# Attention by a forward and a backward running product in place of one and its inverse, in a fused attention and two-layer kernel with a planned order

## The chip, the cores and the metric

One core of one Trainium2 chip runs the whole program. The metric is device time in microseconds, the median of the runs shown; the profile is one execution more. TensorE is called PE here, VectorE DVE, ScalarE ACT, GpSimd POOL, and SP is the queue that issues the transfers.

## The reference

Attention with a decaying state (4 batches, 8 heads, 768 steps, head width 48), then two feed-forward layers over 3072 tokens of width 384, with 1536 and 2048 hidden columns:

```python
for t in range(S):
    cur = np.einsum('bhd,bhe->bhde', u[None] * kt, vt)
    y[:, :, t] = np.einsum('bhd,bhde->bhe', rt, state + cur)
    state = wt[:, :, :, None] * state + np.einsum('bhd,bhe->bhde', kt, vt)
...
a = x @ w_a
b = x @ w_b
x = (a * b) @ w_out
h = np.maximum(x @ w_in, 0.0)
return h * h @ w_out2
```

## The kernel before

**Attention.** 64 steps are a chunk, two chunks of one batch are a pair: 24 pairs, `p0` to `p23`. Transposed r, k and w of a pair lie on 48 + 48 of 112 partitions, one row for each channel and, along the row, 8 heads of 64 steps. `at_scan` (L248) makes the running product of w along each chunk, in `ef`; `at_recip` (L253, four instructions) its inverse, in the second part of `ef`. `at_kr` (L257) multiplies k by the inverse, `at_rr` (L261, one instruction for each chunk) r by the product. From these PE makes the scores `sc` (`at_A`, L288) and the transposed keys `kt` (`at_B`, L299), ACT copies them to `kn`, and PE makes the state update `ds` (`at_C`, L311). `at_C2` (L320 to L324, four steps on DVE) adds the old state and multiplies by the product over the whole chunk, once for each chunk. The bonus term u goes on the diagonal: two multiplications of `nat` (L270), a sum (`at_u2`, L274) and `at_diag` (L278, two). `at_A2` (L294) copies the scores under a mask over it. `at_D` (L332) is the output product `yp`; ACT copies it to `ys`, and it is stored to DRAM as `xd`.

**Feed-forward.** Every product is three float32r products of high and low parts. Layer 1 has 12 weight units, called u0 to u11 here, each 1152 columns for the parts a, b and out of one step f; layer 2 has 11. A unit comes as 64-bit words and is decoded in place: ACT two passes (`dec_z`, `dec_round`), DVE `dec_sign` (L191), `dec_shift` (L195), `dec_add` (L200), ACT `dec_hi`, then `dec_lo` (L209), after which PE may use it. The buffers `z` between these are two. A block of tokens (layer 1: 384, 256, 384, then 512) is loaded as x and split in two (`xl`, L551). Then, for each f: PE makes a and b (`pa`, L358 to L360), ACT copies a, DVE multiplies (L369), ACT takes the high part `gh`, POOL the low part `gl` (L379), and PE adds the step's part into three accumulators `acc` (L385 to L387).

**What sets the order.** `Plan.run` places every step by its due time (`prio`), its costs (`t_dve`, `t_pool`, ...), its needs and the free buffers, and the steps are then issued in this order; each engine and the SP queue works through its own list in order, and semaphores hold what isn't ready. The numbers in `KNOB` set the due times and `ENG` the engines a step may take: `kr`, `gl`, `dg` and `u1` are POOL's, `rr`, `da` (`dec_add`) and `dl` (`dec_lo`) DVE's or POOL's. In the plan POOL's steps and the DVE steps marked `port` exclude each other. Pairs p0 to p2 are block 0 of layer 1, p3 and p4 block 1.

Of the kernel before, what the change touches and what calls it, by code (L numbers as in the profile page):

```python
# [31 lines left out]
T0 = 4
TR, TK, TN = T0, T0 + HC, T0 + 2 * HC
EN = HE + HC
WS = 256.0

KNOB = dict(START=13.52, FIRST=7.12, LEAD=18.8, DEC=4.0, DO=13.32, XO=5.1, X2=-14.73, D2=33.64, LW=15.56, LT=19.97,
            LV=-2.26, LV2=-0.35, LN=7.51, scan=2.25, rec=6.21, kr=-1.09, rr=5.02, u1=-0.24, u2=2.9, dg=-11.72,
            gd=-27.44, A=-3.1, B=4.87, C=-16.56, D=10.05, T2=4.14, EARLY=2.77, WAIT=0)
# [84 lines left out]
def fused_kernel(ctx, tc, tpk, natpk, vpk, v2pk, upk, cst, w1pk, w2pk, out):  # L124
# [319 lines left out]
    def plan_pair(p):  # L444
# [16 lines left out]
        add("scan", {"DVE": 1.27}, K["scan"], lambda e: at_scan(p), [("LT", p)], port=True)
        for k in range(4):
            add(("rec", k), {"DVE": 0.87}, K["rec"] - k, lambda e, k=k: at_recip(p, k), [("scan", p)])
        add("kr", both(0, HC, *ENG["kr"]), K["kr"], lambda e: at_kr(p, e), [("LRK", p), *((("rec", k), p) for k in range(4))],
            port=True)
# [390 lines left out]
```

## Time and profile before

| | |
|---|---|
| median of 3 runs | 999.94 us (999.16 to 1000.58) |
| profiled execution | 998.08 us, span 996.2 us |
| mean granted clock of TensorE | 0.976 |
| PE, DVE, ACT, POOL busy | 940.4 (94%), 479.3 (48%), 384.1 (39%), 441.6 (44%) us |
| chain that ended last, by engine | PE 88%, DVE 5%, DMA 3% |

Busy time is what an engine spent in instructions, matmuls with a modelled end. Stretches with different limits lie under these shares, so the rows further down go by stretch: start-up and first pairs, block 0, and the rest. A row's start less the start before it is the pace of an engine; its own duration is some 0.08 us longer, since instructions overlap at their ends. An entry in brackets is the idle time before an instruction and what ended it.

### The profile page before, as it was taken

The numbers are of one execution on the slowest core, as the hardware profiler recorded it, in microseconds if no ns is written. First come the engines' busy times: TensorE is split into PE (matmuls) and PEld (weight loads), VectorE is DVE, ScalarE is ACT, GpSimd is POOL, SyncE is SP. The second block draws the span as 40 slices with busy tenths as digits, with TensorE's granted clock in tenths as the row PEclk, the third lists the DMA queues.
The fourth block names the chain that finished last, engine by engine and source line by source line (L and its number), as shares of the span: only waits on it lengthen the run. The fifth ranks groups of instructions, "written<-read, shape, count | busy, mean of one in ns | idle before, by whom it ended". The sixth has DMA issues, their size and how long they took to land.

```text
span 996.2 us, 14962 instructions
## 1 busy us (share of the span) xinstructions
PE 940.4 (94%) x5982; PEld 802.0 (81%) x5982; DVE 479.3 (48%) x585; ACT 384.1 (39%) x591; POOL 441.6 (44%) x359
## 2 busy tenths in 40 slices
PE   2668799999999999999999999999999999999997
PEld 2567699999988888888888888888888888888885
DVE  6889988875764444573212688721121211211111
ACT  1677443433422333332332677442233332323322
POOL 6733478886674545544122344333333333333332
PEclk9579899999999999999999999999999999999999
DMA  9995134652632332341111554010010000100001
GB/s 267 335 332 135 59 99 128 178 148 77 166 117 76 108 107 77 94 135 38 40 42 64 191 205 143 1 64 1 6 59 0 33 32 1 64 1 1 32 0 37
DMA packets 57791, 91.89 MB, mean 92 GB/s; under 512 B 23664, under 2 KB 31600, under 8 KB 57712
## 3 DMA queue, kind: packets, MB, share of 16 engines
q1 hardware_dynamic: 57712, 90.84, 29.6%
q8 instruction: 49, 0.80, 0.3%
q14 instruction: 30, 0.25, 0.1%
HBM read 76.66 MB, written 14.16 MB: 91 GB/s over the span
## 4 chain that ended last, share of the span: by engine, by line
PE 88%; DVE 5%; DMA 3%; ACT 1%; issue 1%; SPq 0%; POOL 0%; DVEq 0%; ACTq 0%
PE pa L358 16%; PE pa L360 16%; PE pa L359 16%; PE acc L385 11%; PE acc L387 11%; PE acc L386 11%; PE sc L288 2%; PE yp L332 2%; DVE w L209 1%; DVE z L200 1%; PE kt L299 1%; DMA ef<-in_tpk_dram 1%; PE ds L313 1%; DVE z L195 1%; DMA vs<-in_vpk_dram 1%
## 5 line engine op out<-in xcount | busy, mean ns | idle before, releaser
L379 POOL TENSOR_TENSOR gl<-a,gh 128x512 fp32r<-128x512 f32 (+2 forms) x180 | 235.2, 1308 | 474.4 <-ACT gh L176 469.9
L358 PE MATMUL pa<-xh,w 128*128 128x512 f32 (+2 forms) x792 | 296.3, 374 | 7.7 <-ACT w L176 3.3
L360 PE MATMUL pa<-xh,w 128*128 128x512 f32 (+2 forms) x792 | 295.1, 373 | 7.6 <-DVE w L209 7.6
L359 PE MATMUL pa<-xl,w 128*128 128x512 f32 (+2 forms) x792 | 294.4, 372 | 0.0
L365 ACT ACTIVATE a<-pa 128x512 f32<-128x512 f32 (+2 forms) x180 | 102.3, 569 | 277.8 <-PE pa L360 219.1
L385 PE MATMUL acc<-gh,w 128*128 128x512 f32 (+2 forms) x540 | 205.6, 381 | 0.0
L387 PE MATMUL acc<-gl,w 128*128 128x512 f32 (+2 forms) x540 | 202.7, 375 | 0.0
L386 PE MATMUL acc<-gh,w 128*128 128x512 f32 (+2 forms) x540 | 202.4, 375 | 0.0
L369 DVE TENSOR_TENSOR a<-a 128x512 f32<-128x512 f32 x96 | 67.9, 707 | 253.4 <-ACT a L365 253.4
L176 ACT ACTIVATE gh<-a 128x512 fp32r<-128x512 f32 (+2 forms) x180 | 108.3, 602 | 207.7 <-DVE a L369 161.9
L358 PEld LDWEIGHTS pa<-xh,w 128*128 128x128 f32 x792 | 150.1, 190 | 32.8 <-ACT w L176 4.3
L360 PEld LDWEIGHTS pa<-xh,w 128*128 128x128 f32 x792 | 150.2, 190 | 32.0 <-DVE w L209 9.2
L359 PEld LDWEIGHTS pa<-xl,w 128*128 128x128 f32 x792 | 150.1, 189 | 22.7 <-DVE xl L551 0.3
L369 DVE TENSOR_TENSOR a<-a,pa 128x512 f32<-128x512 f32 (+2 forms) x84 | 51.0, 607 | 140.8 <-PE pa L360 140.4
L385 PEld LDWEIGHTS acc<-gh,w 128*128 128x128 f32 x540 | 101.4, 188 | 17.9
L387 PEld LDWEIGHTS acc<-gl,w 128*128 128x128 f32 x540 | 101.5, 188 | 17.3 <-POOL gl L379 0.4
L386 PEld LDWEIGHTS acc<-gh,w 128*128 128x128 f32 x540 | 101.5, 188 | 16.2
L253 DVE RECIPROCAL ef<-ef 112x128 f32<-112x128 f32 x96 | 82.7, 913 | 0.5
L261 POOL TENSOR_TENSOR ar<-rk,ef 48x512 f32<-48x512 f32 (+1 forms) x48 | 59.0, 1230 | 27.8 <-DVE ef L248 10.0
L294 DVE COPY_PREDICATED ar<-mask,sc 64x512 f32<-64x512 int32 x48 | 35.2, 734 | 39.7 <-PE sc L289 37.7
L278 POOL TENSOR_TENSOR ar<-ident,dg 64x512 f32<-64x512 f32 x48 | 51.5, 1073 | 1.8
L209 DVE TENSOR_TENSOR w<-z,w 128x1152 fp32r<-128x1152 f32 (+1 forms) x22 | 37.2, 1691 | 6.0 <-ACT w L176 6.0
(54 smaller groups left out, 834.3 us busy)
## 6 DMA issues: line engine op xcount, KB each, us to landing
raw<-in_w1pk_dram SPq DMA_DIRECT2D x36, 384.0 KB, 6.8
raw<-in_w2pk_dram SPq DMA_DIRECT2D x32, 384.0 KB, 3.8
rk<-in_tpk_dram SPq DMA_DIRECT2D x24, 448.0 KB, 4.9
nat<-in_natpk_dram SPq DMA_DIRECT2D x24, 384.0 KB, 3.7
v<-in_v2pk_dram SPq DMA_DIRECT2D x24, 384.0 KB, 4.3
ef<-in_tpk_dram SPq DMA_DIRECT2D x24, 227.5 KB, 3.7
vs<-in_vpk_dram SPq DMA_DIRECT2D x48, 96.0 KB, 2.8
xd<-ys SPq DMA_DIRECT2D x48, 96.0 KB, 3.2
```

Of the source, the lines that this page charges most:

```text
L176: nc.scalar.activation(out=out, in_=in_, func=ACTF.Copy, **({} if scale is None else {"scale": scale}))
L253: nc.vector.reciprocal(out=hv(inv(p), C)[:, h0:h0 + 2], in_=hv(ext(p), C + 1)[:, h0:h0 + 2, 1:])
L261: eng(e).tensor_tensor(out=hv(AR[p % 2][rows, c, :], C), in0=hv(RK[p][rows, TR:TK], C), in1=hv(ext(p), C + 1)[rows, :, 0:C], op=ALU.mult)
L358: nc.tensor.matmul(out=out, lhsT=blk(wh, k), rhs=h, start=(k == 0), stop=False)
L359: nc.tensor.matmul(out=out, lhsT=blk(wh, k), rhs=l, start=False, stop=False)
L360: nc.tensor.matmul(out=out, lhsT=blk(wl, k), rhs=h, start=False, stop=(k == KD - 1))
L365: nc.scalar.activation(out=a[:, 0:n], in_=P[:, 0:n], func=func, scale=scale)
L369: eng(e).tensor_tensor(out=a[:, 0:n], in0=a[:, 0:n], in1=b[:, 0:n], op=ALU.mult)
L379: eng(e).tensor_tensor(out=gl[:, 0:n], in0=g[:, 0:n], in1=gh[:, 0:n], op=ALU.subtract)
L385: nc.tensor.matmul(out=o, lhsT=blk(wh, d), rhs=gh[:, 0:n], start=first, stop=False)
L386: nc.tensor.matmul(out=o, lhsT=blk(wl, d), rhs=gh[:, 0:n], start=False, stop=False)
L387: nc.tensor.matmul(out=o, lhsT=blk(wh, d), rhs=gl[:, 0:n], start=False, stop=last)
```

## The change

- The inverse goes. The host sends w a second time, reversed in each chunk, and k, v and the rows of the scores are reversed too. `at_scan` makes two running products, `bwd` and `fwd`, with one small reciprocal between them (of the product over a whole chunk, 8 columns), which starts the forward one. `at_kr` multiplies k by `bwd`. The load of `ef` is 112x1040 in place of 112x520.
- `at_C2` has three steps in place of four; the multiplication of the incoming state is a step of its own, `at_Z`, in place.
- In pairs p0 to p5 (`ENG0`) `kr`, `rr`, `dg` and `u1` are DVE's; the additions `da` of layer 1 are DVE's too. Later pairs keep them on POOL.
- Due times are new, with one for each of p0 to p7, and some steps wait for the same step of the pair before. Block 0 could be computed in two parts, which is off (`APART=0`).

```diff
-EN = HE + HC
+EN = 2 * HE
...
 ENG = dict(kr=("POOL",), da=("DVE", "POOL"), dl=("DVE", "POOL"), rr=("POOL", "DVE"), u2=("DVE",), xs=("DVE",), d2=("ACT",),
-           b2=("ACT",), gl=("POOL",), gh=("ACT",))
+           b2=("ACT",), gl=("POOL",), gh=("ACT",), dg=("POOL",), u1=("POOL",), ds=("DVE",))
+ENG0 = dict(ENG, kr=("DVE",), da=("DVE",), rr=("DVE",), dg=("DVE",), u1=("DVE",))
+NP0 = 6
...
     def at_load(p):
         EF[p] = ap.tile([112, EN], F32, tag="ef", name="ef", bufs=3)
-        nc.sync.dma_start(out=ext(p), in_=tpk[p, :, 2 * HC:])
+        nc.sync.dma_start(out=EF[p], in_=tpk[p, :, 2 * HC:])
...
     def at_scan(p):
-        nc.vector.tensor_tensor_scan(out=ext(p), data0=ext(p), data1=floor[0:112], initial=0.0,
+        first = hv(floor, C + 1)[:, :, 0:1]
+        nc.vector.memset(first[0:112], 1.0)
+        nc.vector.tensor_tensor_scan(out=bwd(p), data0=bwd(p), data1=floor[0:112], initial=0.0,
                                      op0=ALU.mult, op1=ALU.max)
-
-    def at_recip(p, q):
-        h0 = q * 2
-        nc.vector.reciprocal(out=hv(inv(p), C)[:, h0:h0 + 2], in_=hv(ext(p), C + 1)[:, h0:h0 + 2, 1:])
+        nc.vector.reciprocal(out=first[0:112], in_=whole(p))
+        nc.vector.tensor_tensor_scan(out=fwd(p), data0=fwd(p), data1=floor[0:112], initial=0.0,
+                                     op0=ALU.mult, op1=ALU.max)
...
+    def at_Z(p):
+
+        v = VS[p % 2][EV, 0, :]
+        if p % PPB == 0:
+            nc.vector.memset(v, 0.0)
+        else:
+            nc.vector.tensor_tensor(out=hv(v, D), in0=hv(v, D), in1=whole(p)[EV].to_broadcast([D, H, D]), op=ALU.mult)
+
     def at_C2(p):
...
-        nc.vector.tensor_tensor(out=P[EV], in0=P[EV], in1=vs[EV, 0, :], op=ALU.add)
-        nc.vector.tensor_tensor(out=hv(vs[OD, 1, :], D), in0=hv(P[EV], D), in1=fe[EV], op=ALU.mult)
+        z = vs[OD, 1, :]
+        nc.vector.tensor_tensor(out=z, in0=P[EV], in1=vs[EV, 0, :], op=ALU.add)
+        nc.vector.tensor_tensor(out=hv(z, D), in0=hv(z, D), in1=whole(p)[OD].to_broadcast([D, H, D]), op=ALU.mult)
         if p % PPB != PPB - 1:
-            nc.vector.tensor_tensor(out=P[OD], in0=P[OD], in1=vs[OD, 1, :], op=ALU.add)
-            nc.vector.tensor_tensor(out=hv(nx[EV, 0, :], D), in0=hv(P[OD], D), in1=fe[OD], op=ALU.mult)
+            nc.vector.tensor_tensor(out=nx[EV, 0, :], in0=P[OD], in1=z, op=ALU.add)
...
-        if j == 0:
-            q = K["FIRST"] * (i - m)
-        else:
-            q = tau[j - 1] + (tau[j] - tau[j - 1]) * i / m - K["LEAD"]
+        E0 = ENG0 if p < NP0 else ENG
+        q = K.get(f"P{p}", tau[j - 1] + (tau[j] - tau[j - 1]) * i / m - K["LEAD"] if j else 0.0)
...
-        add(("da", u, s), {"DVE": t_dve(n) + 0.08, "POOL": t_pool(n)}, prio, lambda e: dec_add(u, n, e), [("dt", u, s)],
+        add(("da", u, s), both(0, n, *(ENG0 if s == 1 else ENG)["da"]), prio, lambda e: dec_add(u, n, e), [("dt", u, s)],
```

What this does to the order is shown at three places. The first is pair p0, from the first scan on. Before, on DVE (`ef` is the pair's products, `dg` the diagonal, `vs_91` state and v):

```order
L248 SCALAR_TENSOR_TENSOR ef<-ef,floor 112x520 x2
L253 RECIPROCAL ef<-ef 112x128 x4
L274 TENSOR_REDUCE dg<-nat 128x8
L253 RECIPROCAL ef<-ef 112x128 x4
L319 MEMSET vs_91 48x384
```

and, beside it, on POOL (`rk` is r and k of a pair, `ar_89` and `ar_90` the score rows of two pairs):

```order
L270 TENSOR_TENSOR nat<-nat 128x384
L270 TENSOR_TENSOR nat<-nat,u_sb 128x384
L261 TENSOR_TENSOR ar_89<-rk,ef 48x512
L261 TENSOR_TENSOR ar_89<-rk,ef 64x512
L257 TENSOR_TENSOR rk<-rk,ef 112x512
```

Now all of it stands in DVE's list, one after the other:

```order
L263 MEMSET floor 112x8
L264 SCALAR_TENSOR_TENSOR ef<-ef,floor 112x520
L266 RECIPROCAL floor<-ef 112x8
L267 SCALAR_TENSOR_TENSOR ef<-ef,floor 112x520
L339 MEMSET vs_92 48x384
L285 TENSOR_TENSOR nat<-nat 128x384
L285 TENSOR_TENSOR nat<-nat,u_sb 128x384
L289 TENSOR_REDUCE dg<-nat 128x8
L276 TENSOR_TENSOR ar_90<-rk,ef 48x512
L276 TENSOR_TENSOR ar_90<-rk,ef 64x512
L272 TENSOR_TENSOR rk<-rk,ef 112x512
```

Five instructions of POOL moved behind the scans, and eight reciprocals of two pairs are gone.

The second place is the last third of the x of block 0 (`xl`) on DVE. Before, two units are decoded when it comes, `w_487` here and one on POOL, and the third is begun (`raw_200`):

```order
L209 TENSOR_TENSOR w_487<-z,w_487 128x1152
L551 TENSOR_TENSOR xl<-xl,xh 128x3x128
L191 TENSOR_SCALAR raw_200<-raw_200 128x1152
L551 TENSOR_TENSOR xl<-xl,xh 128x3x128
L195 SCALAR_TENSOR_TENSOR z<-z,raw_200 128x1152
L551 TENSOR_TENSOR xl<-xl,xh 128x3x128
L200 ISA z<-raw_200,z 128x2304
```

Now it stands here:

```order
L208 ISA z<-raw_246,z 128x2304
L579 TENSOR_TENSOR xl<-xl,xh 128x3x128
L199 TENSOR_SCALAR raw_253<-raw_253 128x1152
L298 TENSOR_TENSOR ar_91<-anti,dg 64x512
L217 TENSOR_TENSOR w_497<-z,w_497 128x1152
L203 SCALAR_TENSOR_TENSOR z<-z,raw_253 128x1152
L199 TENSOR_SCALAR raw_367<-raw_367 128x1152
L208 ISA z<-raw_253,z 128x2304
L579 TENSOR_TENSOR xl<-xl,xh 128x3x128
```

More decoding lies ahead of x: units u0 and u2 are ready on DVE (u1 on POOL), u3 lacks only its high and low parts (`dec_hi`, `dec_lo`), and u4 is begun.

The third place is the end of the decoding of layer 1 on DVE. Before (`w_1080` is u11):

```order
L209 TENSOR_TENSOR w_1038<-z,w_1038 128x1152
L200 ISA z<-raw_644,z 128x2304
L369 TENSOR_TENSOR a<-a,pa 128x384
L248 SCALAR_TENSOR_TENSOR ef<-ef,floor 112x520
L209 TENSOR_TENSOR w_1080<-z,w_1080 128x1152
L253 RECIPROCAL ef<-ef 112x128 x4
```

Now (`w_1095` is u11):

```order
L217 TENSOR_TENSOR w_1053<-z,w_1053 128x1152
L208 ISA z<-raw_604,z 128x2304
L263 MEMSET floor 112x8
L264 SCALAR_TENSOR_TENSOR ef<-ef,floor 112x520
L266 RECIPROCAL floor<-ef 112x8
L267 SCALAR_TENSOR_TENSOR ef<-ef,floor 112x520
L217 TENSOR_TENSOR w_1095<-z,w_1095 128x1152
```

The scan of p5 stands ahead of the last step of u11 in both, now with two products.

## Rows read from the trace of the kernel before

**Rows 1.** Busy time by stretch: us, then each engine with instructions, PEclk, DMA share, GB/s.

```profile
61.46:144.29 82.83, 70.70 (x452) 64.92 (x453) 73.42 (x71) 45.49 (x58) 41.08 (x29) 0.92 0.43 135
144.29:989.20 844.91, 844.73 (x5194) 715.90 (x5194) 357.85 (x451) 310.29 (x496) 364.60 (x296) 1.00 0.24 73
115.00:120.00 5.00, 4.80 (x43) 4.28 (x44) 3.12 (x5) 3.42 (x4) 1.99 (x2) 0.62 0.01 3
```

**Rows 2.** Timeline of PE: start, us, engine, line, operation, [idle before <-releaser].

```profile
61.46 0.69 PE L358 MATMUL pa<-xh,w 128*128 128x384 f32 x1 [2.96 <-ACT xh L176]
...
115.20 0.69 PE L360 MATMUL pa<-xh,w 128*128 128x384 f32 x1 [3.55 <-DVE w L209]
...
133.16 0.33 PE L358 MATMUL pa<-xh,w 128*128 128x384 f32 x1
```

**Rows 3.** Busy time by stretch, up to the x of block 0 and after it.

```profile
3.78:61.92 58.14, 25.24 (x337) 21.42 (x337) 47.70 (x61) 26.49 (x36) 34.97 (x29) 0.73 0.99 310
61.92:132.25 70.33, 58.20 (x355) 53.38 (x355) 65.11 (x61) 41.91 (x51) 29.27 (x19) 0.91 0.45 142
```

**Rows 4.** Timeline of DVE, from the first scan to the last decode of layer 1.

```profile
3.78 2.38 DVE L248 TENSOR_TENSOR_SCAN ef<-ef,floor 112x520 f32<-112x520 f32 x2 [2.23 <-DMA ef<-in_tpk_dram]
...
37.94 3.37 DVE L253 RECIPROCAL ef<-ef 112x128 f32<-112x128 f32 x4
41.23 1.42 DVE L294 COPY_PREDICATED ar<-mask,sc 64x512 f32<-64x512 int32 x2
42.69 0.58 DVE L320 TENSOR_TENSOR ds<-ds,vs 48x384 f32<-48x384 f32 x1
...
57.81 0.55 DVE L551 TENSOR_TENSOR xl<-xl,xh 128x384 fp32r<-128x384 f32 x1
58.28 0.75 DVE L191 TENSOR_SCALAR raw<-raw 128x1152 int32<-128x1152 int32 x1
58.95 0.55 DVE L551 TENSOR_TENSOR xl<-xl,xh 128x384 fp32r<-128x384 f32 x1
...
61.44 0.56 DVE L551 TENSOR_TENSOR xl<-xl,xh 128x384 fp32r<-128x384 f32 x1 [0.68 <-ACT xh L176]
61.92 1.35 DVE L200 CUSTOM_DVE_ANT_0 z<-raw,z 128x2304 uint16<-128x2304 uint16 x1
63.19 0.75 DVE L191 TENSOR_SCALAR raw<-raw 128x1152 int32<-128x1152 int32 x1
63.86 1.23 DVE L248 TENSOR_TENSOR_SCAN ef<-ef,floor 112x520 f32<-112x520 f32 x1
65.01 1.33 DVE L209 TENSOR_TENSOR w<-z,w 128x1152 fp32r<-128x1152 f32 x1
67.90 0.56 DVE L369 TENSOR_TENSOR a<-a,pa 128x384 f32<-128x384 f32 x1 [1.56 <-PE pa L360]
...
86.38 2.17 DVE L200 CUSTOM_DVE_ANT_0 z<-raw,z 128x2304 uint16<-128x2304 uint16 x1
...
99.94 0.58 DVE L320 TENSOR_TENSOR ds<-ds,vs 48x384 f32<-48x384 f32 x1
...
130.92 1.33 DVE L209 TENSOR_TENSOR w<-z,w 128x1152 fp32r<-128x1152 f32 x1
```

**Rows 5.** Timeline of POOL at three places.

```profile
9.88 0.99 POOL L270 TENSOR_TENSOR nat<-nat,u_sb 128x384 f32<-128x384 f32 x1 [1.88 <-DMA u_sb<-in_upk_dram]
...
86.30 1.04 POOL L379 TENSOR_TENSOR gl<-a,gh 128x384 fp32r<-128x384 f32 x1 [7.43 <-ACT gh L176]
...
99.99 2.70 POOL L200 TENSOR_TENSOR z<-z,raw 128x1152 int32<-128x1152 int32 x1 [1.29 <-DVE z L195]
```

**Rows 6.** Groups by line on POOL up to 61.92 us: busy, mean ns, idle before.

```profile
L261 POOL TENSOR_TENSOR ar<-rk,ef 48x512 f32<-48x512 f32 (+1 forms) x8 | 9.4, 1171 | 3.8 <-DMA rk<-in_tpk_dram 3.3
...
L270 POOL TENSOR_TENSOR nat<-nat 128x384 f32<-128x384 f32 x4 | 4.8, 1199 | 7.0 <-DMA nat<-in_natpk_dram 6.9
```

**Rows 7.** Timeline of ACT, output of pair 2.

```profile
49.76 1.19 ACT L176 ACTIVATE ys<-yp 48x512 f32<-48x512 f32 x2
```

More of the change, by code (lines that the diff above doesn't have):

```diff
@@ L28 @@
 BLOCKS1 = [384, 256, 384] + [512] * 4
+FIRST, APART = 256, 0
 BLOCKS2 = [512] * 6
@@ L187, in dec_round, with dec_sign @@
         copy("ACT", words(u, n)[:, :, 0], words(u, n, U32)[:, :, 0], 2.0 ** -29)
-    def dec_sign(u, n):
+    def dec_sign(u, n, e="DVE"):
         s = words(u, n)[:, :, 1]
+        if e == "ACT":
+            f = words(u, n, F32)[:, :, 1]
+            return copy(e, f, f, 0.0)
         nc.vector.tensor_scalar(out=s, in0=s, scalar1=-2 ** 31, scalar2=None, op0=ALU.bitwise_and)
@@ L277, in at_diag @@
         rows = slice(c * C, c * C + C)
+        if e == "ACT":
+            for h in range(H):
+                nc.scalar.activation(out=AR[p % 2][rows, c, h * C:(h + 1) * C], in_=anti[rows], func=ACTF.Copy,
+                                     scale=DG[p][rows, h:h + 1])
+            return
         eng(e).tensor_tensor(out=hv(AR[p % 2][rows, c, :], C),
-                             in0=ident[rows, rows].rearrange("p (o t) -> p o t", o=1).to_broadcast([C, H, C]),
+                             in0=anti[rows].rearrange("p (o t) -> p o t", o=1).to_broadcast([C, H, C]),
                              in1=DG[p][rows].rearrange("p (h o) -> p h o", o=1).to_broadcast([C, H, C]), op=ALU.mult)
@@ L380, in split_lo, with down @@
         return gl
-    def down(acc, d, w, g, n, first, last):
+    def down(acc, d, w, g, c0, n, first, last, full=None):
         (wh, wl), (gh, gl) = w, g
-        o = acc[d][:, 0:n]
-        nc.tensor.matmul(out=o, lhsT=blk(wh, d), rhs=gh[:, 0:n], start=first, stop=False)
+        o, m = acc[d][:, c0:c0 + n], full if full and first else n
+        nc.tensor.matmul(out=acc[d][:, c0:c0 + m], lhsT=blk(wh, d), rhs=gh[:, 0:m], start=first, stop=False)
         nc.tensor.matmul(out=o, lhsT=blk(wl, d), rhs=gh[:, 0:n], start=False, stop=False)
@@ L461, in plan_pair @@
[L461 to L464, printed above, removed]
+        add("LN", {"DMA": t_dma(384)}, K["LN"], lambda e: at_load_n(p), [("LN", p - 1)], acq=[("nat", p)], lat=DMA_LAT)
+        add("scan", {"DVE": 2.75}, K["scan"], lambda e: at_scan(p), [("LT", p)], port=True)
@@ new lines, in plan_step, with dn @@
+        add(("gl", *k), both(0, n, *(ENG0 if (s, j) == (1, 0) else ENG)["gl"]), early,
+            lambda e: put(("gl", *k), split_lo(box["g", *k], box["gh", *k], n, e)),
+            [("gh", *k), *(("gl", *b) for b in before)], rel=[("a", k)], port=True)
+        def dn(d):
+            acc = box.setdefault(("acc", s, j), {})
+            if d not in acc:
+                acc[d] = new_acc(d)
+            down(acc, d, part(w_down), (box["gh", *k], box["gl", *k]), c0, n, f == 0 and start, f == nf - 1, fill and NB)
@@ L648, in consts @@
+        plan_out(2, j, NF2 - 1, n, tau2[j + 1] - dt, out[:, :, offs2[j]:offs2[j + 1]])
     def consts(e):
@@ L679, in finish @@
         for d in range(KD):
-            down(acc, d, w, (gh, gl), NG, first, last)
+            down(acc, d, w, (gh, gl), 0, NG, first, last)
     def store(acc, dst):
```

184 lines of the change are left out of this document (103 added, 81 removed).

## The prediction, on record before the run

> **What bounds the kernel now.** I first read busy time by stretch. From 144.29 to 989.20 us PE is busy 844.73 of 844.91 us [rows 1]: nothing that DVE or POOL saves there can show, only matmuls could, and their number doesn't change. So the 18 later pairs, each with fewer DVE steps, are worth nothing, and the whole case lies before 144.29 us. In block 0 (61.46 to 144.29) PE is idle 82.83 - 70.70 = 12.1 us [rows 1]. Its timeline says on what: on the last step of decoding a weight unit, `w` of L209, 3.55 us at 115.20 [rows 2]. So the second thing to see is the queue of DVE. Its last decode, of u11, starts at 130.92 and takes 1.33 us [rows 4]; PE starts u11 at 133.16 [rows 2] and never stops afterwards. **The time is set by when u11 is decoded**, and this by two stretches of DVE's list: up to the x of block 0 (start of its last part 61.44, the next instruction at 61.92), and from there to 132.25. DVE is busy 47.70 of 58.14 and 65.11 of 70.33 us in them [rows 3].
>
> **Prices.** An undisturbed instruction costs the distance to the next start [rows 4]: scan 1.15 (63.86 to 65.01), four reciprocals 3.29 (37.94 to 41.23), a masked copy 0.73 (two from 41.23 to 42.69), a 384-wide tensor-tensor step 0.47 (57.81 to 58.28), `dec_sign` 0.67, the other 1152-wide decoding steps 1.27 (61.92 to 63.19), a state step about 0.59. The 512-wide steps that come to DVE aren't in its trace; the line through 384 (0.47) and 1152 (1.27) gives 0.60. The 8-column reciprocal with its memset is not there either: 0.2 a pair, between 0.1 (nearly all start-up) and 0.3; six of them, so it hardly matters.
>
> **DVE's list before, by these prices.** To x: 4 scans 4.6, 16 reciprocals 13.1, 8 masked copies 5.9, 16 state steps 9.5, 4 sums 1.9, a memset 0.4, 3 signs 2.0, 6 other decoding steps 7.6, 3 steps of x 1.4: 46.4. It took 58.1, so 11.7 went on waiting and collisions, nearly all waiting (58.14 - 47.70 = 10.4). From x to u11: 2 scans 2.3, 5 reciprocals 4.1, 2 copies 1.5, 4 state steps 2.4, a sum 0.5, 9 signs 6.0, 27 decoding steps 34.3, 10 products of a and b 4.7: 55.8. It took 70.3: 5.2 waiting, and 65.1 - 55.8 = 9.3 in which instructions ran long.
>
> **What made them run long** is POOL. The same `dec_add` form takes 1.35 us at 61.92 and 2.17 at 86.38, where a `gl` of 1.04 us runs beside it [rows 4, 5]: 0.8 us for one `gl`. It isn't each time: in the timeline of this stretch 5 of 9 `gl` did it, so 0.45 on the mean; the rest of the 9.3 falls on POOL's attention and decoding steps. At 99.94 a state step, with one input in PSUM, keeps its 0.58 us beside a POOL addition of 2.70 [rows 4, 5]. The Trainium skill ("SBUF — State Buffer", section Who interferes with whom) has it that a DVE instruction with two SBUF inputs and a POOL instruction that reads SBUF shut each other out for the whole of the one that came first, and that one SBUF input at most is safe. The two rows agree with it. By that rule the steps that come to DVE, all with two SBUF inputs, are open to collisions, and each of the ten `gl` could cost its whole 1.0 us, 10 in place of 4.5 in the sum below.
>
> **The change, to x.** DVE's list now: 8 scans 9.2, 4 small reciprocals 0.8, nineteen 512-wide steps (8 `rr`, 4 `kr`, 7 `dg`) 11.4, eleven 384-wide ones (8 of `nat`, 3 of the new `Z`) 5.2, 6 copies 4.4, 9 state steps 5.4, 4 sums 1.9, a memset 0.4, 5 signs 3.4, 10 decoding steps 12.7, x 1.4: 56.2. The first scan needs 455 KB of `ef`; before, the two scans of p0 and p1 ran back to back from 3.78 [rows 4], so their two halves of that size were there by 4.9, and I take 4.4. Without a wait x is at 60.6. Waits that I can follow: the second step on `nat` stands seventh at 7.8, and u_sb came at 9.88 before [rows 5], now some 0.5 later behind 190 KB more, so 2.6; r and k of p1, 0.7; the two `z` buffers and ACT's high part (u4 can't start before u2 is finished) 2.5. Sum: x at 60.6 + 5.8 = **66.4**, 4.5 later than 61.92. The other path to x agrees: the output of p2 left ACT from 49.76 [rows 7], 11.7 before 61.44; now the state of p2 is finished at about 51.7, its output starts some 2.8 later, and 54.5 + 11.7 is 66.2. Bounds for the waits: 3 (the first alone) and 11.7, as before.
>
> **From x to u11.** Now 4 scans 4.6, 2 small 0.4, six 512-wide 3.6, three 384-wide 1.4, 4 copies 2.9, 6 state steps 3.5, a sum 0.5, 7 signs 4.7, 23 decoding steps 29.2, 10 products 4.7: 55.5, as much as before; two units more are nearly done at x, and that pays for what came from POOL. Added: the wait for the first product of PE, whose first matmuls run at the low clock (1.56 at 67.90 before [rows 4]), 2.3 now. Collisions: POOL keeps 10 `gl`, 0.45 each, 4.5, and two `dec_lo` that stand beside copies and state steps and cost nothing by the row at 99.94. Bounds: 0, and all of POOL's time there, 15.2. Sum: 66.4 + 55.5 + 2.3 + 4.5 = **u11 at 128.7**, where it was at 132.25.
>
> **On PE.** PE takes up u11 right after two matmul groups of u10, and waits for it about 2 us; after a wait of that kind before, the granted clock of the 5 us was 0.62, so partly at 1.2 in place of 2.4 GHz [rows 1, 2], and the nine matmuls behind it cost 1.3 more. Three accumulating matmuls fewer are left at that point, -0.5. So u11's work counts from 128.7 + 0.1 + 1.3 - 0.5 = 129.6 against 133.16: -3.6. The rest I cost at nothing: the larger load of `ef` in later pairs, `Z` and the longer guard on ACT are hidden by PE's full queue; without that cover each pair would pay its DVE steps. SP's list has one small load more and the doubled `ef`, four of them by x, 0.93 MB or 3.0 us at the 310 GB/s of this stretch [rows 3]; p3's is issued well ahead of its scan.
>
> The profiled execution took 998.08 us, 1.9 below the median of 999.94. The difference of 3.6 goes on the median: 999.94 - 3.6 = **996.3 us**.
>
> **Rivals.**
> - **PE becomes the bound.** If POOL, with little left, hardly collides, u11 is at 124.2. PE needed 133.16 - 61.46 = 71.7 us from its first block-0 matmul, 12.1 of it idle and 1.3 at the low clock, so 58.3 without them: 66.5 + 58.3 = 124.8, less 0.5. Then -8.9, 991.1 us. For it: POOL's time after x falls from 29.27 [rows 3] to 15. Against: `gl` still falls beside decoding.
> - **DVE waits for loads (slower).** The pair's first steps on POOL waited 6.9 us for `nat` and 3.3 for `rk` [rows 6], while DVE went on with reciprocals. Now such a wait, at the same place in the list, stops DVE and all decoding behind it. If the stretch to x loses 11.7 as before and not 5.8, 5.9 come on top: 1002.2 us. It decides from 3.6 more waiting, 9.4 in all. For it: SP's loads ran at 310 GB/s, share 0.99 [rows 3], and `ef` adds to them.
> - **The lock (slower).** Nearly every step beside POOL's `gl` now has two inputs in SBUF, and all of POOL's 15.2 us after x is paid by DVE: u11 at 139.4, 996.3 + 10.7 = 1007.0 us. It loses from 8.1 of collisions on. Against: 4 of 9 `gl` cost nothing. This is how the time would come out if the rule of the Trainium skill named above met every one of them.
> - **It doesn't do what it says.** DVE's list merely trades reciprocals for POOL's steps (55.8 against 55.5 after x), PE's other waits, for PSUM and for products, pace block 0, and nothing comes of it: 999.9 us.
>
> **How the numbers follow.** A difference under 0.2%, 2.0 us, can't be told from none. My forecast has 0.46; with collisions of 3 to 8 and waits of 4 to 8 its own range is 993.5 to 1001, which gives faster 0.35, same 0.10, slower 0.01. PE as the bound 0.12, all faster. Loads 0.17: slower 0.13, same 0.04. Lock 0.12: slower 0.11, same 0.01. No effect 0.13: same 0.12, slower 0.01. Together faster 0.47, same 0.27, slower 0.26. The range 992.0 to 1003.5 leaves out most of the lock, the upper end of the loads and half of the first rival, about 0.2.
>
> **What would show it.** x's last part at 66 on DVE (62 before); u11's decode ending near 129; PE starting u11's part before 131 and saturated from there on; waits of PE in block 0 well under 12 us; DVE's 1152-wide steps nearer 1.35 us on the mean. If x comes after 70, the loads have it; if x is at 66 and u11 after 133, the collisions; if PE shows idle time after 145 us, the new order broke the cover that I rely on, and the forecast is wrong whatever the opening does.

## The result, and the profile after

| | before | after |
|---|---|---|
| median | 999.63 us (4 runs beside it) | 1007.08 us (1005.33 to 1008.09, 4 runs) |
| ratio | 1 | 1.0073, 95% interval 1.0061 to 1.0086 |
| profiled execution, span | 998.08, 996.2 us | 1006.95, 1005.2 us |
| PE, DVE, ACT, POOL busy | 940.4, 479.3, 384.1, 441.6 us | 945.3, 476.7, 383.4, 421.7 us |
| last product of layer 1 decoded (u11, end of `dec_lo`) | 132.25 us | 137.92 us |

Slower by 0.73%, where 996.3 us was forecast. DVE is busy 2.6 us less and POOL 19.9 us less; PE, with the same matmuls, 4.9 us more. First the stretches that answer to [rows 1] and [rows 3]: up to the x of block 0, from there to u11, block 0 on PE, the rest, and six microseconds at the end of block 0.

```profile
5.44:68.23 62.79, 24.49 (x305) 20.48 (x305) 59.80 (x83) 29.19 (x37) 2.65 (x1) 0.82 0.97 306
68.23:137.92 69.69, 61.79 (x396) 57.40 (x396) 65.48 (x69) 38.58 (x50) 25.82 (x13) 0.89 0.45 144
67.39:148.46 81.07, 72.32 (x467) 66.39 (x467) 74.08 (x83) 41.84 (x56) 28.94 (x16) 0.86 0.42 134
148.46:998.20 849.74, 848.96 (x5211) 719.30 (x5210) 342.67 (x434) 310.87 (x497) 389.10 (x296) 1.00 0.25 78
138.00:144.00 6.00, 5.36 (x16) 4.85 (x17) 3.80 (x7) 0.90 (x2) 1.02 (x1) 0.50 0.01 3
```

From 148.46 on PE is busy 848.96 of 849.74 us: as forecast, most of it is decided ahead of that. Block 1 itself starts only 4.2 us later (144.29 before), while the span is 9.0 us longer: behind that mark the change has 17 more matmuls left (5211 against 5194, accumulating ones of block 0, some 0.17 us each, 2.9 in all) and 0.6 us more of idle time, and 1.3 us stay open. So u11 is the better mark. From the first scan to x DVE stood idle only 62.79 - 59.80 = 3.0 us; from x to u11 it was busy 65.48 of 69.69 us, where 60.0 was forecast. In the last row PE works 5.36 us at 0.50, the lower of its two levels (1.2 GHz), which the kernel before did not at this point (1.00 from 120 to 140 us). The timeline of PE, against [rows 2]:

```profile
67.39 0.69 PE L383 MATMUL pa<-xh,w 128*128 128x384 f32 x1 [6.09 <-ACT xh L181]
...
114.58 0.69 PE L385 MATMUL pa<-xh,w 128*128 128x384 f32 x1 [1.66 <-DVE w L217]
...
135.49 0.44 PE L383 MATMUL pa<-xh,w 128*128 128x384 f32 x1 [0.61 <-ACT a L390]
...
137.98 0.69 PE L385 MATMUL pa<-xh,w 128*128 128x384 f32 x1 [1.88 <-DVE w L217]
...
141.23 0.69 PE L383 MATMUL pa<-xh,w 128*128 128x384 f32 x1 [0.64 <-ACT a L390]
```

x comes 5.9 us later (67.39 against 61.46). PE waits for u8's and u11's last decoding step (L217 is `dec_lo` now) 1.66 and 1.88 us. DVE's timeline, against [rows 4]:

```profile
5.44 1.24 DVE L264 TENSOR_TENSOR_SCAN ef<-ef,floor 112x520 f32<-112x520 f32 x1 [3.74 <-DMA ef<-in_tpk_dram]
...
52.20 2.31 DVE L347 TENSOR_TENSOR vs<-vs,ef 48x384 f32<-48x384 f32 x1
...
67.76 0.55 DVE L579 TENSOR_TENSOR xl<-xl,xh 128x384 fp32r<-128x384 f32 x1
...
73.56 0.56 DVE L394 TENSOR_TENSOR a<-a,pa 128x384 f32<-128x384 f32 x1 [1.43 <-PE pa L385]
...
97.45 1.57 DVE L199 TENSOR_SCALAR raw<-raw 128x1152 int32<-128x1152 int32 x1
...
105.42 2.51 DVE L347 TENSOR_TENSOR vs<-vs,ef 48x384 f32<-48x384 f32 x1
...
131.69 2.16 DVE L208 CUSTOM_DVE_ANT_0 z<-raw,z 128x2304 uint16<-128x2304 uint16 x1
...
136.59 1.33 DVE L217 TENSOR_TENSOR w<-z,w 128x1152 fp32r<-128x1152 f32 x1
```

L347 is the second state step, L199 `dec_sign`, L208 `dec_add`. The state step takes 0.55 us alone, and here 2.31 and 2.51; a sign 0.75, and here 1.57; `dec_add` 1.35, and here 2.16. What stands beside these four on POOL (and a `gl` at 91.17 that is read further down):

```profile
51.45 2.65 POOL L217 TENSOR_TENSOR w<-z,w 128x1152 fp32r<-128x1152 f32 x1 [49.93 <-ACT w L181]
...
91.17 4.38 POOL L406 TENSOR_TENSOR gl<-a,gh 128x384 fp32r<-128x384 f32 x1 [2.82 <-ACT gh L181]
...
96.64 1.77 POOL L406 TENSOR_TENSOR gl<-a,gh 128x384 fp32r<-128x384 f32 x1 [1.08 <-ACT gh L181]
...
104.81 2.71 POOL L217 TENSOR_TENSOR w<-z,w 128x1152 fp32r<-128x1152 f32 x1 [3.17 <-ACT w L181]
...
131.14 1.51 POOL L406 TENSOR_TENSOR gl<-a,gh 128x384 fp32r<-128x384 f32 x1 [4.25 <-ACT gh L181]
```

Each long DVE instruction begins inside one of POOL's and ends 0.4 to 1.2 us after it: 52.20 + 2.31 = 54.51 against 51.45 + 2.65 = 54.10; 105.42 + 2.51 = 107.93 against 104.81 + 2.71 = 107.52; 97.45 + 1.57 = 99.02 against 98.41. That is in each case some 0.15 us less than the instruction takes alone (0.55, 0.75, 1.35 us): it is held back until POOL is about through, and then does its work.

### The profile page after: what moved, and what is told of

It reads as the page before. It is cut to its first block, busy times and chain, and to the rows that moved or that the text cites. A ratio compares the mean times of both kernels' runs of the same rounds, so it can differ in the third digit from the quotient of the medians.

```text
span 1005.2 us, 14964 instructions
## 1 busy us (share of the span) xinstructions
PE 945.3 (94%) x5982; PEld 806.0 (80%) x5982; DVE 476.7 (47%) x602; ACT 383.4 (38%) x591; POOL 421.7 (42%) x318
## 4 chain that ended last, share of the span: by engine, by line
PE 84%; DVE 8%; DMA 3%; issue 2%; ACT 1%; SPq 0%; DVEq 0%; ACTq 0%
PE pa L383 15%; PE pa L385 15%; PE pa L384 15%; PE acc L413 11%; PE acc L415 11%; PE acc L414 11%; DMA raw<-in_w1pk_dram 2%; PE yp L357 2%; PE sc L308 2%; DMA rk<-in_tpk_dram 1%; DVE z L208 1%; DVE vs L347 1%; DVE raw L199 1%; DVE ar L314 1%; DVE z L203 1%
## 5 line engine op out<-in xcount | busy, mean ns | idle before, releaser
L406 POOL TENSOR_TENSOR gl<-a,gh 128x512 fp32r<-128x512 f32 (+2 forms) x180 | 246.8, 1371 | 484.5 <-ACT gh L181 483.0
L181 ACT ACTIVATE gh<-a 128x512 fp32r<-128x512 f32 (+2 forms) x180 | 108.3, 602 | 226.9 <-DVE a L394 172.9
L276 POOL TENSOR_TENSOR ar<-rk,ef 48x512 f32<-48x512 f32 (+1 forms) x36 | 47.0, 1304 | 20.4 <-PE yp L358 12.8
L298 POOL TENSOR_TENSOR ar<-anti,dg 64x512 f32<-64x512 f32 x36 | 41.7, 1157 | 3.4 <-DVE floor L263 1.7
L357 PE MATMUL yp<-ar,vs 112*48 112x64 f32 x384 | 30.2, 237 | 12.3 <-DMA xl<-xd 9.7
L357 PEld LDWEIGHTS yp<-ar,vs 112*48 112x48 f32 x384 | 25.9, 135 | 19.4 <-issue 17.4
```

The source lines that it names most:

```text
L181: nc.scalar.activation(out=out, in_=in_, func=ACTF.Copy, **({} if scale is None else {"scale": scale}))
L357: nc.tensor.matmul(out=P[OD, cs], lhsT=vs[0:112, 0, es], rhs=ar[0:112, 0, cs], start=True, stop=True)
L406: eng(e).tensor_tensor(out=gl[:, 0:n], in0=g[:, 0:n], in1=gh[:, 0:n], op=ALU.subtract)
```

## The experiments

Three theories. **A, collisions:** DVE pays for POOL's instructions, at steps that the prediction costed at nothing. **D, the list:** DVE simply has more to do than was counted, or the parts of the change (products, engines, due times) don't fit each other. **C, PE:** waits and a low clock on PE take what DVE saves. All runs, with the times of their profiles:

| run | median us | ratio to before (95%) | first `pa` of block 0 | u11 ready |
|---|---|---|---|---|
| before | 998.72 to 1000.19 | 1 | 61.46 | 132.25 |
| the change | 1007.08 | 1.0073 (1.0061 to 1.0086) | 67.39 | 137.92 |
| e2_state_psum | 1003.04 | 1.0028 (1.0014 to 1.0042) | 68.02 | 136.83 |
| e3_lo_dve | 1008.08 | 1.0094 (1.0067 to 1.0121) | 75.62 | 137.33 |
| e5_gl_dve | 1007.12 | 1.0074 (1.0057 to 1.0091) | 67.56 | 135.88 |
| e13_psum_gl | 1005.42 | 1.007 (1.0054 to 1.0087) | 66.68 | 134.49 |
| e14_no_gl | 997.11 | 0.9981 (0.997 to 0.9991) | 67.65 | 130.73 |
| e15_before_no_gl | 993.63 | 0.9952 (0.9937 to 0.9968) | 63.07 | 128.08 |
| e9_products_only | 1023.08 | 1.0246 (1.0229 to 1.0263) | 86.16 | 148.85 |
| e8_due_only | 1003.49 | 1.0037 (1.0023 to 1.0051) | 70.44 | 135.42 |
| e7_engines_only | 1012.67 | 1.0132 (1.0115 to 1.0149) | 77.72 | 141.52 |
| e1_engines_back | 1016.7 | 1.017 (1.0149 to 1.019) | 67.61 | 142.29 |
| e6_due_back | 1010.2 | 1.0104 (1.0087 to 1.0121) | 73.43 | 144.21 |
| e11_due_engines | 1005.08 | 1.0065 (1.0048 to 1.0082) | 80.14 | 140.87 |
| e10_psum_sign | 993.95 | 0.9941 (0.9925 to 0.9958) | 68.98 | 126.31 |
| e12_sign_kept | 994.14 | 0.9953 (0.9938 to 0.9968) | 68.41 | 125.93 |
| e16_psum_dg | 1001.07 | 1.0027 (1.0014 to 1.004) | 69.11 | 132.36 |
| e17_psum_u1 | 1001.93 | 1.0035 (1.0021 to 1.005) | 71.39 | 133.88 |

### The state step through PSUM

```diff
-        nc.vector.tensor_tensor(out=z, in0=P[EV], in1=vs[EV, 0, :], op=ALU.add)
-        nc.vector.tensor_tensor(out=hv(z, D), in0=hv(z, D), in1=whole(p)[OD]...
+        nc.vector.tensor_tensor(out=P[EV], in0=P[EV], in1=vs[EV, 0, :], op=ALU.add)
+        nc.vector.tensor_tensor(out=hv(z, D), in0=hv(P[EV], D), in1=whole(p)[OD]...
```

> The changed kernel with one thing undone: the first state step writes back to PSUM and the second reads it there, so that the second (L347) has one SBUF input in place of two; every engine's order stays as it is. Theory A, POOL's instructions shut out DVE steps with two SBUF inputs: the two long ones of block 0's opening (2.31 us at 52.2 and 2.51 at 105.4, each beside a POOL dec_lo) fall to 0.56, the last decode comes 3.7 us earlier (137.9 to about 134.2) and the time falls from 1007.1 to 1002.5 to 1005. Theory B, DVE's list is simply too long and collisions only move to the next instruction: the long step is another one, 1006 to 1008. Theory C, the loss lies in PE's order and its low clock after u11: no change, 1006.5 to 1007.5.

Measured 1.0028 against 1.0073: 4.5 us of the 7.3 are back, give or take 1.9 (4.0 between the medians), with the same instructions in the same order. DVE's timeline of this run, then POOL's:

```profile
52.85 0.56 DVE L347 TENSOR_TENSOR vs<-ds,ef 48x384 f32<-48x384 f32 x1
...
54.03 1.31 DVE L341 TENSOR_TENSOR vs<-vs,ef 48x384 f32<-48x384 f32 x1
...
105.63 0.56 DVE L347 TENSOR_TENSOR vs<-ds,ef 48x384 f32<-48x384 f32 x1
...
107.28 1.65 DVE L208 CUSTOM_DVE_ANT_0 z<-raw,z 128x2304 uint16<-128x2304 uint16 x1
...
109.13 1.30 DVE L199 TENSOR_SCALAR raw<-raw 128x1152 int32<-128x1152 int32 x1 [0.20 <-ACT z L181]
...
135.50 1.33 DVE L217 TENSOR_TENSOR w<-z,w 128x1152 fp32r<-128x1152 f32 x1
```

```profile
52.23 2.69 POOL L217 TENSOR_TENSOR w<-z,w 128x1152 fp32r<-128x1152 f32 x1 [50.71 <-ACT w L181]
...
105.01 2.71 POOL L217 TENSOR_TENSOR w<-z,w 128x1152 fp32r<-128x1152 f32 x1 [3.17 <-ACT w L181]
```

The state step has one input in PSUM now, as it had before the change, and takes 0.56 us beside the same POOL instruction (52.23 to 54.92, 105.01 to 107.72) that made it 2.31 and 2.51. Part of the lock moves on to the next instruction with its inputs in SBUF (the state multiplication L341 at 54.03, `dec_add` at 107.28, the sign at 109.13), and x comes 0.6 us later than in the change (68.02), after more waits on DVE (4.5 us against 3.0), so u11 is only 1.1 us earlier, not 3.7. The rest comes behind it: in 149 to 900 us the group of this step, first of the change, then of this run, is

```profile
L347 DVE TENSOR_TENSOR vs<-vs,ef 48x384 f32<-48x384 f32 x19 | 15.8, 834 | 0.6
```

```profile
L347 DVE TENSOR_TENSOR vs<-ds,ef 48x384 f32<-48x384 f32 x19 | 10.6, 559 | 0.6
```

834 ns on the mean against 559; PE's idle time from block 1 to 998 us, 0.8 us in the change, is nil here. Theory A holds for this step; how the 4.5 us divide between these places is open, beyond the 1.1 and 0.8.

### Low parts and `dec_lo` on DVE, or low parts left out

```diff
-ENG0 = dict(ENG, kr=("DVE",), ...
+ENG0 = dict(ENG, kr=("DVE",), ..., dl=("DVE",))     (e3: dec_lo of layer 1)
+ENG0 = dict(ENG, kr=("DVE",), ..., gl=("DVE",))     (e5: gl of block 0; e13: and the state step through PSUM)
```

> The changed kernel with dec_lo of layer 1 on DVE alone, so that POOL keeps only gl in block 0 (the order is planned anew). Theory A (collisions): three dec_lo of 1.3 us come to DVE, 3.9, and the two collisions of 3.7 us go: 1006 to 1008. Theory B (length of DVE's list): 3.9 us more, 1010 to 1012.

> The changed kernel with gl of block 0 on DVE (12 steps of about 0.47 us, ten of them before u11), order planned anew; POOL keeps three dec_lo. Theory A (collisions): 4.7 us come, some seven collisions of 0.8 (5.6 us) go, 1005 to 1007.5. Theory B (length): 4.7 us more, 1010 to 1013.

> The changed kernel with the state step through PSUM and gl of block 0 on DVE: POOL hardly works beside DVE's decoding any more. gl alone on DVE brought nothing (1007.1) though u11 came 2 us earlier, and the state step alone brought 4 us. Theory A (what is left of the loss after the state step is gl beside signs): 10 gl of 0.47 come to DVE, their collisions go, u11 by 133.5 and 999 to 1001 us. Theory Q (gl in DVE's list comes late, since it stands behind decoding there, and PE's accumulating matmuls wait for it): 1003 us or more, with waits of PE on gl in block 0.

e3 and e5 are level with the change, e13 (1.007) is behind e2. In e3 the new order brings x to 75.62, and u11 is only 0.6 us earlier. In e5 and e13 u11 is 2.0 and 2.3 us earlier than in the change and in e2, and nothing comes of it: PE waits 4.7 us ahead of an attention product at 122.16 and 120.76 (0.49 and 0.96 there), and then for `gl`, now in DVE's list, which is theory Q of e13. PE in e13 (2.94 us at 138.28 in e5):

```profile
136.88 0.44 PE L415 MATMUL acc<-gl,w 128*128 128x384 f32 x1 [2.82 <-DVE gl L406]
```

So these three don't price the collisions. Two more leave `gl` out, so that DVE's list stays as it is (the third product reads `gh`), in e2's kernel (e14) and in the kernel before (e15):

```diff
-lambda e: put(("gl", *k), split_lo(box["g", *k], box["gh", *k], n, e))
+lambda e: put(("gl", *k), box["gh", *k] if (s, j) == (1, 0) else split_lo(box["g", *k], box["gh", *k], n, e))
```

> The changed kernel with the state step through PSUM (1003.0 us), and the low part gl of block 0 left out: its third products read gh in its place, so POOL has nothing to do there but three decoding steps, and DVE's list stays as it is. It prices the collisions with gl by themselves. By the trace of the changed kernel five signs, one score row, one dec_add and one state multiplication run 0.7 to 0.8 us long beside a gl, 6.6 us in all. Theory A (these collisions are the rest of the loss): u11 decoded by 131, 994 to 998 us. If PE, which still waits for the same units, takes the gain up elsewhere (low clock after each wait): 999 to 1002. If the collisions only filled time in which DVE would have waited: within 2 us of 1003.

> The kernel before with the gl of block 0 left out in the same way. The prediction put 0.45 us on each of ten gl there, 4.5 of the 9.3 us that DVE's instructions ran long. If so, 995 us. If gl costs as much there as in the changed kernel (6.6): 993. If the waits for the first units hide it: 998 or more.

e14 is 0.9981 against e2's 1.0028: 4.7 us, with u11 6.1 us earlier. e15 is 0.9952 against 1: 4.8 us, u11 4.2 earlier. DVE in e14, then in e15:

```profile
67.63 0.56 DVE L579 TENSOR_TENSOR xl<-xl,xh 128x384 fp32r<-128x384 f32 x1 [0.76 <-ACT xh L181]
...
96.07 0.76 DVE L199 TENSOR_SCALAR raw<-raw 128x1152 int32<-128x1152 int32 x1
...
104.05 2.67 DVE L208 CUSTOM_DVE_ANT_0 z<-raw,z 128x2304 uint16<-128x2304 uint16 x1
...
129.40 1.33 DVE L217 TENSOR_TENSOR w<-z,w 128x1152 fp32r<-128x1152 f32 x1
```

```profile
63.05 0.56 DVE L551 TENSOR_TENSOR xl<-xl,xh 128x384 fp32r<-128x384 f32 x1 [0.56 <-ACT xh L176]
...
126.75 1.33 DVE L209 TENSOR_TENSOR w<-z,w 128x1152 fp32r<-128x1152 f32 x1
```

The sign at 96.07 is 0.76 us (1.57 at 97.45 in the change). At 104.05 `dec_add` is still 2.67 us: POOL's `dec_lo` is beside it. PE waits for no `gl` in block 0, neither before nor in e2, so what is gone is DVE's collisions: ten `gl` are worth 0.5 us each in both kernels, close to the 0.45 of the prediction. Without them the change, its state step through PSUM, is still 997.11 against 993.63: the `gl` are not what sets the two kernels apart.

### The three parts of the change, apart

e9 is the products with the engines and due times of before (and with the new waits for the pair before, the change's last point, which no run takes out), e8 the due times alone, e7 the engines alone; e1, e6 and e11 leave one part out each:

```diff
+ENG0 = ENG                                                  (in the change: e1, e9)
-        q = K.get(f"P{p}", ...
+        q = ... if j else K["FIRST"] * (i - m)              (in the change, with KNOB and decoding due as before: e6, e9)
+ENG0 = dict(ENG, kr=("DVE",), da=("DVE",), rr=("DVE",), dg=("DVE",), u1=("DVE",))    (in before: e7, e11)
-KNOB = dict(START=13.52, FIRST=7.12, ...
+KNOB = dict(START=13.73, LEAD=19.82, ...                    (in before, with p0 to p7 and decoding due as now: e8, e11)
```

> The changed kernel with the engines of before in all pairs and in decoding (kr, dg, u1 on POOL, rr on POOL or DVE, da on DVE or POOL), the two products and the due times kept. If it was the move of POOL's steps to DVE that lost, DVE's list up to u11 loses 21 reciprocals (17 us) against 6 scans and small ones (8 us) and gets POOL's collisions back, about as many as before (9 us): 992 to 1000, not slower than before. If the two products or the new due times lose by themselves: 1004 to 1010.

> The changed kernel with the due times of the kernel before (no times of its own for p0 to p7, decoding due from the start of block 0 again); the two products, three state steps and the steps moved to DVE stay. Theory A (collisions: instructions with two inputs in SBUF beside POOL cost 4 us, by the run with the state step in PSUM, and the rest is the list itself): the due times hardly matter, within 3 us of 1007. Theory D (the due times are what fits the move to DVE; the list of DVE is the bound and its order decides): over 1012 us, x of block 0 after 70. Theory O (the new due times are what costs the time; they let decoding in ahead of the pairs): under 1003 us, x before 66.

> The kernel before with one part of the change alone: kr, rr, dg and u1 of p0 to p5 and the additions of layer 1 on DVE; inverse, four state steps and due times as before. From the run of the changed kernel with its engines put back (10 us slower): if that gain belongs to the move alone, 990 us. If DVE's list sets the end (it gets 19 steps of 0.6 and 8 of 0.47 to x, 15 us, of which at most 10.4 of idle time can take them), x of block 0 5 us later and more, over 1004 us. If it only trades waiting for work: within 2 us of 1000.

> The kernel before with the new due times alone (KNOB, p0 to p7, decoding from 0.2 us on); inverse, four state steps and engines as before. If the due times are the loss that the run with engines put back showed (1016.7): over 1010 us, with decoding ahead of the pairs and x of block 0 after 66. If that loss belongs to the two products (their load of twice the size before the first scan, and r and k behind it): within 3 us of 1000.

> The two products, their three state steps and the larger load alone, on the engines and with the due times of the kernel before. Known: all three parts 1007.1, without the due times 1010.2, engines alone 1012.7, due times alone 1003.5, products and due times 1016.7. If the products are a gain in DVE steps (eight reciprocals of 0.82 less a pair of scans) where POOL keeps its steps: under 999 us. If POOL's steps now wait for the second scan and its larger load, and DVE gains what it cannot use: 1000 to 1008. If the loss of 1016.7 was theirs: over 1010.

> The kernel before with the new due times and the move of steps to DVE together, but the inverse and four state steps of before. If the parts simply add: 1003.5 + 1012.7 - 999.5 = 1016.7. If the due times were made for the move: under 1012.7, and near 1010. The difference from 1007.1 is then what the products are worth in the place where they were put; by the DVE list (before u11 six reciprocal groups of 3.3 less six second scans of 1.15 and small ones, some 12 us) 10 us and more, less if DVE waits there anyway.

That the parts add up was wrong (1016.7 expected for e11, 1005.08 measured), and e1, above both of its ranges, shows that with the products the move of engines is a gain of 10 us; e6 lies between its theories. Each part alone loses: 1.3% (engines), 0.4% (due times), 2.5% (products). Alone, the engines bring the last part of x to 77.70, 16.3 us after before's 61.44. DVE's idle time up to there fell from 10.4 to 4.1 us, but it was busy 70.42 us in place of 47.70, 22.7 more and not 15; some 4.5 of this are two pairs of 512-wide steps that ran 3.5 and 3.8 us beside a `dec_lo` of POOL, where such a pair takes 1.4:

```profile
48.45 3.54 DVE L263 TENSOR_TENSOR ar<-rk,ef 48x512 f32<-48x512 f32 x2
...
62.83 3.77 DVE L280 TENSOR_TENSOR ar<-ident,dg 64x512 f32<-64x512 f32 x2
...
77.70 0.56 DVE L555 TENSOR_TENSOR xl<-xl,xh 128x384 fp32r<-128x384 f32 x1
```

The products alone do worst, and their trace shows a load: DVE's scan of p3 in this run, and in the change.

```profile
41.55 1.24 DVE L263 TENSOR_TENSOR_SCAN ef<-ef,floor 112x520 f32<-112x520 f32 x1 [10.99 <-DMA ef<-in_tpk_dram]
```

```profile
40.08 1.24 DVE L264 TENSOR_TENSOR_SCAN ef<-ef,floor 112x520 f32<-112x520 f32 x1
```

The doubled `ef` of p3 is waited for 10.99 us (7.06 in e1), and x comes only at 86 us. DVE reaches this scan at 30.56 here, and 9.5 us later in the change, where the load is just there; SP issues it at 31.55 and at 28.98. Most of the wait is thus DVE's being early. The rival "DVE waits for loads" is real in the two runs with the products and the old engines, and absent with the new ones. What holds this load until about 40 us was not tried. The products, with those waits between pairs, are therefore worth +24.6 us on before's engines and due times, +13 on the new due times alone (1.017 against 1.0037), -3 with the engines (1.0104 against 1.0132, intervals that overlap), and nothing that can be told with both (1.0073 against 1.0065), where e11's expectation had 10 and more. e2 shows part of what took it: 1.0028 against 1.0065, -3.7 us, once the state step keeps out of POOL's way.

### DVE's list shortened

e10 takes the signs of layer 1 to ACT, with the state step through PSUM; e12 is the same with a bias of -0.0. Both compute layer 1 with weights that lack their signs: against the expectation the zero doesn't keep the sign, and the bias doesn't bring it back. Their times are read as those of the same instructions, though what signs do to PE's clock was not separated.

```diff
+ENG0 = dict(ENG, kr=("DVE",), ..., ds=("ACT",))
```

> The changed kernel with the state step through PSUM (1003.0 us) and, besides, the sign of each unit of layer 1 taken on ACT (an activation by 0.0, 1.13 us, for 0.67 on DVE and for the 0.75 more that it took beside gl). The signs multiply to a zero of the right sign, so the result is the same. If DVE's list up to u11 sets the end: 7 signs of 0.67 after x and 5 collisions of 0.75 go, 8 us at most, of which ACT's longer chain gives some back: 996 to 999 us, under the kernel before. If ACT becomes the bound (its passes stand in the chain of each unit): 1003 us or more. If PE's own waits for the first units set the pace: about 1001.

> The run with signs on ACT and the state step through PSUM, with a bias of -0.0 at the activation, for the weights' signs; otherwise the same instructions. Time: as there, 994 us (992 to 996) if signs or no signs do not matter to it; if the instruction is longer with a bias, or PE's power draw under real signs lowers the granted clock, 996 or more.

They take 8.7 and 7.5 us less than e2, and less than the kernel before. PE over 40 us of block 0, and u11 on DVE:

```profile
80.00:120.00 40.00, 40.00 (x293) 38.88 (x292) 36.81 (x38) 32.55 (x41) 20.12 (x11) 1.00 0.57 162
```

```profile
124.98 1.33 DVE L217 TENSOR_TENSOR w<-z,w 128x1152 fp32r<-128x1152 f32 x1
```

PE never stops from 80 to 120 us and u11 is there at 126.31: this is near the rival "PE becomes the bound", priced 991.1 at u11 = 124.2, though PE still waits 2.17 us for u11 at 126.37. With u11 2.1 us later than in the price, 993.95 and 994.14 come near it, so here the road from u11 to the time was right, as far as weights without signs can tell. e16 and e17 keep the output and take the diagonals to ACT, and the `nat` steps to POOL besides:

```diff
+ENG0 = dict(ENG, kr=("DVE",), da=("DVE",), rr=("DVE",), dg=("ACT",), u1=("DVE",))     (e16; e17: u1=("POOL",))
```

> The changed kernel with the state step through PSUM and the diagonals of p0 to p5 on ACT (8 activations of one row block each in place of one step of DVE): 7 steps of 0.6 leave DVE's list to x and 5 after it, 7 us. If the length of DVE's list sets the time: 997 to 1000 us, and the output is that of the reference. If ACT's longer list (2.65 us for each diagonal in the plan) delays the units' high parts: 1003 and more.

> The same with the two steps on nat of p0 to p5 on POOL besides, which is empty until 51 us: another 8 steps of 0.47 leave DVE's list to x, 3.8 us. If the list sets x: x by 64, and 995 to 998 us. If POOL's new steps collide with DVE's (two inputs in SBUF on both sides): as much as they take off, or more, 1000 us or over.

Both miss: level with e2, though u11 is 4.5 and 3.0 us earlier. e17's x is not there by 64 but at 71.39. In e16 PE, what it waits for on ACT, what ACT waits for on DVE, and the clock over the next ten microseconds:

```profile
130.46 0.69 PE L383 MATMUL pa<-xh,w 128*128 128x384 f32 x1 [4.05 <-ACT w L181]
```

```profile
129.24 1.16 ACT L181 ACTIVATE w<-z 128x1152 fp32r<-128x1152 f32 x1 [3.81 <-DVE z L208]
```

```profile
127.87 1.33 DVE L208 CUSTOM_DVE_ANT_0 z<-raw,z 128x2304 uint16<-128x2304 uint16 x1
```

```profile
130.00:140.00 10.00, 8.59 (x62) 7.84 (x63) 8.32 (x13) 5.29 (x17) 3.17 (x3) 0.69 0.24 80
```

PE waits 4.05 us for ACT's high part of u11 (L181), but ACT itself had stood idle for 3.81 us until DVE's `dec_add` of u11, which has both scans of p5 ahead of it in DVE's list (in the change it stands before them). So this wait comes from the order of DVE's list, theory D, and not from ACT's longer list. Then the ten microseconds run at 0.69 of the clock, which is theory C, and PE waits 2.08 us more at 278.08. In e14 the same stretch, with waits of 1.44 and 0.64 us, keeps the full clock:

```profile
130.00:140.00 10.00, 8.58 (x79) 7.63 (x80) 9.54 (x17) 3.02 (x6) 0.00 (x0) 1.00 0.27 68
```

No run with the reference's whole computation beats the kernel before; e2 and e16 come nearest.

## Why the prediction was wrong

The sum gave u11 at 128.7 and PE 3.6 us ahead of before; measured were u11 at 137.92 (+9.2) and an end 7.45 us behind. By its steps:

- **What bounds.** Right in the main: most lies before block 1, DVE's last decoding step releases PE in the change, and over the runs u11 and the time go together (126 us gives 0.994, 149 gives 1.025), though not to the microsecond: e16 has u11 where before has it and is 2.7 us slower, and e6 has it 1.9 us after e1 and is 6.6 us faster. For the kernel before it was read too strictly: there u11 was ready at 132.25 and PE came to it at 133.16 without a wait [rows 2], so what PE lost it had lost on earlier units.
- **x at 66.4.** Nearly right, by luck: the errors cancel. Measured 68.23 (the instruction behind x): the first scan at 5.44, not 4.4, +1.0; waits 3.0, not 5.8, -2.8; two products with reciprocal and memset 2.84 us a pair (12.77 to 15.61 on DVE), not 2.5, and small gaps, +1.8; the state step at 52.20, +1.8.
- **From x to u11, 62.3.** Measured 69.69. The list 55.5 holds to 1.2 us, 0.7 of it by the same 2.84 a pair. Waits were 4.2, not 2.3: 1.43 for the first product of PE, 1.55 for another at 124.19, 0.48 for `z`, the rest small gaps.
- **Collisions 4.5.** This is the step that failed. DVE's instructions ran 8.8 us long here. "Two `dec_lo` that stand beside copies and state steps and cost nothing by the row at 99.94" was wrong: that row showed a state step with one input in PSUM, and the change had just put the second state step's input into SBUF. It cost 1.96 us at 105.42, and 1.76 ahead of x; the other `dec_lo` behind x (75.81) did cost nothing. The plan doesn't mark these state steps `port`, so it lets POOL run beside them. The prediction quoted the rule that says so, from the Trainium skill ("SBUF — State Buffer", section Who interferes with whom), and applied it to `gl` but not to the changed line; the trace agrees, 2.51 us against 0.56 in e2. The remaining 6.8 us fell beside `gl` and POOL's `nat` step, 2.3 more than 4.5; e14 has 6.1 for the `gl` at u11, of which 4.7 show in the end. By experiment, e14 takes most of both kinds of collision away and is 9.2 us faster than the change (0.9981 against 1.0073), where the sum had 4.5 for them: so some 4.7 of the 10.8 us that the forecast was off are collisions.
- **PE, 1.3 for the clock.** Mis-sized: 5.36 us of work at 0.50, so 2.7 us lost, +1.4.
- **Sum of the errors:** 1.8 (x) + 1.2 + 1.9 + 2.0 + 2.3 + 1.4 = 10.6 of the 10.8 us between 996.3 and 1007.08. They are read from single traces; only the collisions were tried by themselves. That the terms nearly fill the gap is in part chance: between the two profiled executions, from which they come, the forecast misses by 12.5 us (998.08 - 3.6 against 1006.95). Of the other 1.9, PE's wait at 141.23 (0.64) and its idle time behind 148.46 (0.6 more than before) are 1.2; the rest is open.
- **Rivals.** "The lock" gave 1007.0, and its sign came (x near 66, u11 after 133), but by another account: 15.2 us of collisions with no other error. Measured were 8.8 after x, with other terms late as well; its mechanism is the one that e2 shows, its size is not. "Loads" did not occur in the change and did in e9 and e1. "No effect" by the engines' move fails: alone it costs 1.3%.

The trace of before already showed the collision that was put at nothing. DVE, then POOL:

```profile
111.44 3.71 DVE L209 TENSOR_TENSOR w<-z,w 128x1152 fp32r<-128x1152 f32 x1
```

```profile
111.28 2.65 POOL L200 TENSOR_TENSOR z<-z,raw 128x1152 int32<-128x1152 int32 x1 [6.08 <-ACT w L176]
```

A POOL addition of the same kind as the one at 99.99 [rows 5] held a DVE step with two inputs in SBUF for 2.4 us here (3.71 against 1.33), and the 3.55 us that PE waits at 115.20 [rows 2] end with this step. The row at 99.94 alone could not tell whether POOL costs nothing or PSUM had spared that step.

## What to carry to other kernels

Ask of every edited line which memories its inputs lie in, and what runs on POOL at that moment: here a state step that reads PSUM was free beside POOL (0.56 us), and the same step from SBUF, begun beside POOL's instruction, waited until that was through (2.31 and 2.51 us). A planned order with its engines and loads is one object: three parts that each lose 0.4 to 2.5% alone make 0.7% together, so neither a sum of parts nor the removal of one prices another. And a wait ahead of a saturated stretch can cost twice, once as idle time and once in the clock behind it.

## What was not expected of the hardware

- `dec_sign`, an operation with one tensor input, is held back by `gl` too: 1.57 us against 0.75 (97.45 and 125.93 among others). It does 1152 columns in 0.75 us, where the two-input steps take 1.35. The trace of before has it too (1.57 at 76.41). The Trainium skill ("SBUF — State Buffer", section Who interferes with whom) has it that such one-input operations can run in a mode that takes the shared ports, and calls one SBUF input safe only outside such a mode, a condition that the prediction left out; the rows agree with it.
- POOL is held back as well: a `gl` that took 1.04 us at 86.30 before [rows 5] took 4.38 at 91.17 in the change, beside a row of DVE steps with two inputs in SBUF.
- The low clock does not follow every wait: after 1.88 us PE worked 6 us at 0.50 in the change, after 1.44 in e14 none.
